# Six output tiles in place of four, under a fixed order of tasks

## The chip, the cores and the metric

The kernel runs on one core of one Trainium2 chip. The metric is the device time of one execution in microseconds (us), of which the median over several runs is taken. A span inside a profile runs from the first to the last instruction of the program.

## The reference

Attention over four batches of eight heads, 768 positions of width 64, followed by a gated matrix product over the 3072 resulting rows.

```python
# per batch and head; block = 32, window = 16, nb = 24
k_sum = k.reshape(B, H, nb, block, D).max(axis=3)
v_sum = v.reshape(B, H, nb, block, D).mean(axis=3)
scores_l = scale * q @ k.T                    # kept where |i - j| < window
scores_s = scale * q @ k_sum.T + log(block)   # 24 block summaries, always kept
a = softmax(concat([scores_l_masked, scores_s]))
x = a @ concat([v, v_sum])                    # to [3072, 512]
out = maximum(x @ w1, x @ w2) @ w_out         # 512 -> 1024 -> 512
```

The last line is computed in another form: with `wd = w2 - w1`, max(x w1, x w2) w_out is x (w1 w_out) + relu(x wd) w_out. The kernel forms the product w1 w_out once (tile `w1o`).

## The kernel before

The program is written as a list of about 680 *tasks*. A task is one operation, or one short run of matmuls, on one engine: a load or store (SP's DMA queue), a cast, a run of transposes, a copy out of PSUM. Tasks are registered by `op` in the order of the Python code and get numbers by that. Nothing is emitted then. The string `ORDER` is the written-out result of an earlier planning: each word is a letter for the engine (P TensorE, A ScalarE, D VectorE, G GpSimd, S SyncE), a task's number, and, after a colon, the slots of the buffers that the task is the first to write. `Plan.run` walks through the string and emits each task as it comes. The durations given to `op` are a planner's costs; `run` does not read them, except to see which engines may do a task.

Two consequences matter. An engine executes its own tasks strictly in the order of the string. Between engines, the layer beneath sets the waits, from what has been recorded *earlier* in the string: a task waits for earlier-recorded tasks that wrote what it reads, or that use the buffer it overwrites. So the order in which two tasks of different engines stand in the string decides which of them may have to wait for the other when they touch the same buffer.

Buffers come from `Ring`s. A ring is a number of equal slots; the word in `ORDER` says which slot a new buffer takes. The ones that matter here:

- `osr`: the output tiles `o`, [128, 512] in f32. One task "copy out" (ScalarE or VectorE, line 685, emitted at line 410) fills a tile from PSUM; one task "store" (lines 692 and 694) sends it to the output over SP's DMA queue, on which the loads of k, q and v stand too.
- `banks`: the eight PSUM banks. A group of scores (`scores`, matmuls at line 501) takes two adjoining banks, one for each of its two heads' halves; so do a pair of k and q transposes ("turn", line 434), the values (line 543) and the transposes of x (line 575). A hidden or output product takes one.
- `kqb`, `kx`, `qx`, `pb`, `g`, `land`: casts of k and q, their transposed forms, the exponentials, the rectified hidden rows, and the landing tiles of loads.

The work of a batch: load k, q, v into `land`; cast to bf16; transpose k and q on TensorE (L434); place them ("place k", "place q", copies at L410 from PSUM); block maxima of k on VectorE (L454); scores (L501); exponential on ScalarE (L515); mask on VectorE (L509); values (L543), normalised on VectorE (L549, L552); transposes of x (L575). `maxout` then does, for each group of 256 rows, four hidden products (L660) with their relu (L406 or L408) and two or three output products of 128 rows each (L674 with `w1o`, then L681 twice with `wo`), copied out and stored. The string weaves the products of one batch between the attention of the next, so that TensorE has work while the other engines prepare.

Each core's SP queue works in order: a store is issued when the DMAs ahead of it in the queue have been issued.

Of the kernel before, what the change touches and what calls it, by code (L numbers as in the profile page):

```python
# [12 lines left out]
F32 = mybir.dt.float32  # L13
# [8 lines left out]
    "G32:0,0 S39:0 P79:0,0 G7 G8 D81:0,0 P70:2,0 A92:2 S14:4 G9 A72:2,0 D82:0 P94:4,0 G101:3 S16:5 "  # L22
    "A96:1,0 D3 G10 D83 P103:6,0 S42:6 A69:0 D97:1 G102:1 P71:0 S43:7 A76:0 D84 P104:0 D98 D73:0 G78:2 "
    "A109:1 D105:3,0 G93:3 P80:0 A85:2 D75 P95:0 D74 D106:0 A100:3 P86:2 S62:1 P90:6 D99 A87:0 D107 D108 "
    "P88:0 P110:4 A91:1 D15:0,0 D18 P24:2 A89:2 D20 S52:3 P114:6 D21 A22 D19 A25 P112:0 A111:3 D17:0 "
    "S65:0 D26 A28 P33:3 D27 P116:4 D29 A34 A115:4 D30 P126:2 D31 S53:2 D35 A113:5 G45:0 D117:0 P121:6 "
    "D118:0,0 A49:1 D122:1 G48:0 P119:0 D127:2 D123:1,0 P46:4 S146:4,0 A120:0 D128:0 P124:6 A47:1,0 P50:0 "
    "D125 P131:2 D44:0 A64:0 P460:6 S147:0 D51:0 G63:0 P458:7 A461:0 D132:0 P446:4 D55:1 A59:0 D133:0 "
    "P449:5 S150:5,0 D459 P60:0 P56:2 P455:6 D61:0 A57:0 D66:0 P136:0 P452:7 D67:0 S153:6,0 D137:1 P456 "
    "D138:0 S152:0 P134:2 P129:0 D58:0 P447 S151:0 P453 D54:0 A448:0 S154:7 A130:1 P450 D135 G218:0 "  # L30
    "S156:1 A219:1 P464:4 D457:0 G163:1,0,0,0 G245:2 A451:0 D454:0 S148:0,0 P221:0,0 P139:2 P220:0 P476:6 "
    "D11:0 A140:2 D465 S149:0 A222:0,0 P462:5 D477:1 G257:3 A226:0 P480:7 D223:1 G258:1 A246:0 P482:2 "
    "D224 D463 A481 P141:3 D225 P259:0,0 A483 S175:2,0 P260:0 P227:5 D261:2,0 P478:7 A228:0 D142:2 P484:2 "
    "D143:0 A479 G155:0,0 P248:5,0 D262:0 P247:0 P144:3 A253:2 P471:7 D265:1 S170:3,0 A249:1,0 P485 D229 "
    "A145 P472 D263 D251 D250:1 G157:0 P486 P500:0 D487:0 G230:3 S161 P164:1 P489:5 A231:1 S174:0 D160 "
    "S162 A165 P494:6 D159 A501:2 A167 P232:3,0 P233:0 D264 P490 A234:3,0 D166 G187:0,0,0,0 D168 S169 "
    "A238:3 P473 D235:0 S173:4,0 A495 P496:2 S171:0 D236 D252 D237 D474:1 P266:0 A497 P242:3 P491 D158 "
    "S178:6 A243:2 S180:5 P498:6 D492:2 A267:3 S172:0 P239:2 D499 P269:4 P502:7 A240:5 S493 D268 P507:0 "
    "D244 A270:1 D241 P503 D271 P272:1 P284:3 P254:5 D273:0 D285:1 P504 D274:2,0 S176:7,0 A255:4 D286:0,0 "
    "P508 A505:3 D256 P275:1 A295:0 P278:5 G179:0,0 P287:3 D276:2 P466:7 D279:0 A307:2 D277:0 D288:1 P509 "  # L40
    "S177:0 D280:0 G294:3 D289:0 P281:1 G321:1 P467 S475 D282:2 D283:0 S201:1,0 G181:0 P296:5,0 A510:2 "
    "P290:3 P297:0 A298:0,0 P292:1 D291:3 S197:0,0 P468 A302:0 G306:3 D293 P188:0 S200:0 G322:0 P309:3,0 "
    "P323:5,0 S511 P308:0 A469:1 P516:1 D310:3,0 A325:2,0 S506 P514:2 G334:2 D191 A517:1 D311:1 P518:7 "
    "G333:1 A314:3 S194:6,0 D515 G186 P512:1 A519 S184 D185 P335:3,0 P324:0 A513 P336:0 D326:0 P536:2 "
    "S195:0 A329:1 D341:2 S199:3,0 P520:7 A189 A337:1,0 D313 P530:1 S183 D192 A537:2 D312 D339 D327 "
    "P532:5 D328 A531 D338:1 S198:0 A190 P330:3 P315:1 D300 P521 D299:0 G370:3 A316:0 P552:6 D340 D301 "
    "A331:3 D317 P522 D182 A553:0 P525:0 A523:2 D332 P303:1 A533 P345:3 D193 S204:5 P548:6 A304:5 S488 "
    "S196:0 P534:7 A549 S524 D305 P543:5 A535 P318:1 P342:6 P544 A319:2 P526 A343:1 D320 S202:4 P545 "
    "A346:4 S470 D344 P527 A546:3 P357:1 P351:6 A528:0 P354:3 P550:5 D352:0 A371:1 D355:1 S529 D353:1,0 "
    "P538:0 D358:2 G382:0 A551 D359:2,0 A383:2 P554:6 G205:0,0 D356:0 P561:7 A555 D347 P372:1,0 P385:3,0 "  # L50
    "P373:0 A374:2,0 P384:0 G409:3 P562 D378:1 A386:0,0 G397:2 P360:5 D390:0 P348:1 A410:1 P563 G203:0 "
    "D349:0 D361:2 D350:0 P556:3 D564:2 G211:1,0,0,0 S208 G209 P363:1 P557 D362:0 S206 S547 D364:1 P539 "
    "D365:0 P411:4,0 D387:1 P366:6 G207 P412:0 P368:1 A367:0 P558 D369 P540 A398:0 D559:1 P584:6 A413:3,0 "
    "S560 G210 S565 P568:7 A417:3 D585:1 P588:1 D376 D541:0 P602:2 D375:0 S542 P566:3 D569:0 A603:2 D377 "
    "P586:6 D567 P590:4 D389 A587 D414:0 P212:5 P379:2 D214 P400:6,0 D589 P399:0 A380:3 P604:0 D401:1,0 "
    "P570:1 A405:2 D381 P572:2 A213 D388 A605 D402:1 P574:3 A571 D573 A591 P592:6 D216 A215 D403 D404 "
    "P575 D415 D416 D217 P421:0 P394:4 P579:7 A422:0 P576 A395:2 P580 D577:3 P391:0 D396 S578 P406:4 "
    "P418:2 P593 A407:1 P581 A419:5 D408 P594 A582:1 D420 P597:4 A392:4 D423 P606:5 A595:2 D393 P598 A607 "
    "P433:2 P439:0 P424:6 D434:0 P599 D435:0,0 D440:2 P608:5 D425:1 A600:0 D426:1,0 P610:2 D441:0 A609 "
    "P436:3 P427:6 P430:0 P615:5 D428:0 D437:1 D429:0 P611 D438:0 D431:2 P616 D432:0 P444:6 P442:3 A445:3 "  # L60
    "P617 D443 P612 P674:0 D613:3 P644:1 S614 P628:3 A645:0 S601 P660:4 A618:3 P622:6 S619 S583 P669:7 "
    "D623:1 P624:2 P620:1 A625 P664:5 D621 P638:6 P640:2 D639 P626:1 D661:2 D641 P658:6 D627 P633:4 A659 "
    "P642:2 P634 D643 P662:1 P651:6 D663 P646:2 P656:1 P652 A657 P635 P665 A636:0 P653 P629 D654:3 P666 "
    "S655 S637 P647 A667:1 P630 S668 S596 P648 D631:3 P675 S632 A649:0 P670 P676 S650 P671 A677:1 D672:2 "
    "S678 S673 "
)

# [35 lines left out]
class Plan:  # L103
# [8 lines left out]
    def op(self, engine, us, fn, read=(), write=(), change=(), touch=(), behind=(), prio=0.0, label="",  # L112
           port=False, lanes=(0, 1)):
        t = Task()
        t.port, t.lanes = port, lanes
        t.engine, t.us, t.fn, t.label = engine, us, fn, label
        t.on = us if isinstance(us, dict) else {engine: us}
        t.prio = (prio, len(self.tasks))
        t.new, t.behind = [*write, *change], behind
        t.deps = {w for b in (*read, *change) for w in b.writers}  # L120
        for b in t.new:
            b.writers.append(t)
        for b in (*read, *touch, *t.new):
            b.users.append(t)
        self.tasks.append(t)
        return t
# [20 lines left out]
def kernel(  # L147
# [14 lines left out]
    nc = tc.nc  # L162
# [11 lines left out]
    op = plan.op  # L174
# [4 lines left out]
    def tiles(name, n, shape, dt):  # L179
        return [const.tile(shape, dt, name=f"{name}{i}") for i in range(n)]  # L180
# [18 lines left out]
    xtr = Ring(list(range(2 * NG)))  # L199
    xt_tile = const.tile([128, 2 * NG, KC, GT], BF16, name="xt")  # L200
    gr = Ring(tiles("g", 3, [128, FC, GT], BF16))
    osr = Ring(tiles("o", 4, [128, d_model], F32))
    wd = [Buf(Ring([t])) for t in tiles("wd", 4, [128, KC, 256], BF16)]
    w1br = Ring(tiles("w1b", 2, [128, KC, 256], BF16))
    w1b = [Buf(w1br) for _ in range(4)]
# [114 lines left out]
    def load_v(b, prio, gap, on):  # L320

        vb, parts = Buf(vbr), [Buf(Ring([None])) for _ in range(2)]
        vx_part[b] = [Buf(Ring([None])) for _ in range(2)]
        for n in range(2):
            f = Buf(land)
            view = lambda f=f: f.ap[:, 0:1536].rearrange("p (h m d) -> p h m d", h=4, d=D)
            op("SP", 3.6, lambda view=view, n=n: nc.sync.dma_start(
                out=view().rearrange("p h m d -> p (h m) d"),
                in_=v[b, 4 * n:4 * n + 4].rearrange("h (m r) d -> r (h m) d", r=128)),
               write=[f], behind=v_spread[b - 1], prio=prio + gap * n, label=f"load v{b}{n}")  # L330
            copy(on, lambda view=view, n=n: (
                vb.ap[:, :, 4 * n:4 * n + 4, 0:D].rearrange("p m h d -> p h m d"), view()),
                 read=[f, amean_in], write=[vb, parts[n]], prio=prio + 1, label=f"cast v{b}{n}")
        return vb, parts
# [259 lines left out]
    def load_w12(half, prio, prio_t):  # L594
        fs = []
        for w in (moe_w1, moe_w2):
            f = Buf(land)
            fs.append(f)
            op("SP", 2.75, lambda f=f, w=w: nc.sync.dma_start(
                out=wide(f), in_=w.rearrange("(c p) n -> p c n", p=128)[:, :, 512 * half:512 * half + 512]),  # L600
               write=[f], prio=prio, label=f"load w{half}")
        for n in (2 * half, 2 * half + 1):
            split_w12(n, fs, prio + 10 * (n % 2), prio_t)
# [22 lines left out]

    def load_wo(half, prio):
        f = Buf(land)
        op("SP", 2.75, lambda: nc.sync.dma_start(
            out=wide(f), in_=moe_w_out.rearrange("(c p) n -> p c n", p=128)[:, 4 * half:4 * half + 4, :]),  # L630
           write=[f], prio=prio, label=f"load wo{half}")
        for i in range(2):
            copy({"ACT": 1.05, "POOL": 1.05, "DVE": 0.65}, lambda i=i: (wo[2 * half + i].ap[:], wide(f)[:, 2 * i:2 * i + 2]),
                 read=[f], write=[wo[2 * half + i]], prio=prio + 400, label=f"wo {2 * half + i}")
# [147 lines left out]
```

## Time and profile before

| what | before |
|---|---|
| median of 4 runs | 173.05 us (172.38 to 173.88) |
| the profiled execution | 172.57 us |
| its span | 170.8 us |
| TensorE (PE) busy | 148.4 us, 87% |
| VectorE (DVE) busy | 113.1 us, 66% |
| ScalarE (ACT) busy | 92.1 us, 54% |
| GpSimd (POOL) busy | 42.5 us, 25% |
| mean granted TensorE clock | 0.987 |
| copies into `o` | 14 on ScalarE, 11 on VectorE |
| stores of 128 rows, 256 KB | median 2.5 us from issue to landing |

"Busy" is the time in which an engine executes; idle time of an engine costs something only where another one waits for it. The profile's chain of waits starts at the last instruction and goes back, at each step, to what released it. Views in order of time give the start, the length, the engine and line, the tiles written and read, and in brackets the idle time before and what ended it.

### The profile page before, as it was taken

The page shows a single profiled execution, that of the slowest core. Times are in us where ns is not written, and L with a number is a line of the kernel's source. Part 1 is how long each engine was busy: PE and PEld are TensorE (multiplying, and loading weights), DVE is VectorE, ACT ScalarE, POOL GpSimd, SP SyncE. Part 2 cuts the span into 40 slices and gives each one's busy share as a digit, 9 for nine tenths or more (in the row PEclk, how much of TensorE's full clock was granted, in tenths as well). Part 3 has the DMA queues.
Part 4 walks back from the last instruction along what each step waited for, and adds up shares of the span by engine and source line. Part 5 has one row for each costly group of instructions (what it writes and reads, how often), then busy time and mean ns, then how long its engine had stood idle before and what let it go on. Part 6 is the DMA issues. An engine that isn't in the chain of part 4 may idle for free.

```text
span 170.8 us, 5170 instructions
## 1 busy us (share of the span) xinstructions
PE 148.4 (87%) x2229; PEld 98.2 (57%) x2256; DVE 113.1 (66%) x204; ACT 92.1 (54%) x126; POOL 42.5 (25%) x63
## 2 busy tenths in 40 slices
PE   0237948999999999989899989999999999999992
PEld 0125626647846656567665654788556657876451
DVE  1647899689796887769996549488965661353110
ACT  3287997518764787087797860826666232110220
POOL 7643036106353002880100559500000000000000
PEclk9999996999999999999999999999999999999998
DMA  5998999999999699999999914640010003300065
GB/s 170 367 312 163 285 401 387 384 378 349 215 283 308 126 294 220 290 347 356 268 212 278 273 48 95 165 135 6 0 65 0 0 4 123 127 0 0 0 246 184
DMA packets 42071, 33.57 MB, mean 197 GB/s; under 512 B 25889, under 2 KB 36033, under 8 KB 42049
## 3 DMA queue, kind: packets, MB, share of 16 engines
q1 hardware_dynamic: 42048, 33.25, 68.5%
q8 instruction: 17, 0.28, 0.7%
q14 instruction: 6, 0.04, 0.1%
HBM read 25.17 MB, written 6.29 MB: 184 GB/s over the span
## 4 chain that ended last, share of the span: by engine, by line
PE 68%; DMA 16%; DVE 5%; ACT 4%; issue 3%; SPq 2%; POOL 0%; ACTq 0%; POOLq 0%
PE banks L681 22%; PE banks L660 20%; PE banks L674 11%; DMA land<-in_moe_w_dram 7%; DMA land<-in_q_dram 6%; PE banks L501 4%; PE banks L543 3%; PE banks L644 3%; DMA out_dram<-o 3%; PE banks L434 3%; SPq L305 2%; ACT kx L410 1%; PE banks L575 1%; DVE ks L454 1%; ACT pb L515 1%
## 5 line engine op out<-in xcount | busy, mean ns | idle before, releaser
L660 PE MATMUL banks<-xt,wd 128*128 128x256 bf16 x384 | 46.7, 274 | 0.1
L681 PE MATMUL banks<-wo,g 128*128 128x512 bf16 (+1 forms) x185 | 42.5, 370 | 1.9 <-issue 1.7
L660 PEld LDWEIGHTS <-wd 128*128 128x128 bf16 x384 | 37.2, 98 | 8.2
L515 ACT ACTIVATE pb<-banks,bias 128x1024 bf16<-128x1024 f32 x24 | 25.6, 1111 | 7.7 <-PE banks L501 6.9
L681 PEld LDWEIGHTS <-g 128*128 128x128 bf16 x200 | 18.4, 98 | 18.6
L406 ACT ACTIVATE g<-banks 128x512 bf16<-128x512 f32 x29 | 16.9, 598 | 20.7 <-PE banks L660 20.5
L410 POOL CAST kqb<-land 128x768 bf16<-128x768 f32 x19 | 16.4, 878 | 34.2 <-DMA land<-in_k_dram 28.6
L674 PE MATMUL banks<-w1o,xt 128*128 128x512 bf16 (+1 forms) x90 | 23.5, 370 | 0.6 <-issue 0.2
L434 PE MATMUL banks<-identity,kqb 64*128 64x64 bf16 x384 | 10.6, 202 | 11.9 <-DVE kx L236 4.7
L408 DVE TENSOR_SCALAR g<-banks 128x512 bf16<-128x512 f32 x19 | 12.8, 687 | 10.9 <-PE banks L660 10.9
L454 DVE TENSOR_REDUCE ks<-kx 128x24 bf16<-128x768 bf16 x16 | 15.1, 947 | 4.0 <-ACT kx L410 3.9
L434 PEld LDWEIGHTS <-kqb 64*128 64x128 bf16 x384 | 7.8, 101 | 15.6 <-ACT kqb L410 4.8
L410 ACT COPY o<-banks 128x512 f32<-128x512 f32 (+1 forms) x14 | 8.0, 571 | 15.4 <-PE banks L681 9.1
L552 DVE TENSOR_TENSOR xs<-banks,inv 128x512 bf16<-128x512 f32 x24 | 15.8, 679 | 0.3
L410 DVE COPY o<-banks 128x512 f32<-128x512 f32 (+1 forms) x11 | 7.3, 665 | 12.8 <-PE banks L681 11.7
L410 ACT CAST kqb<-land 128x768 bf16<-128x768 f32 x12 | 9.9, 835 | 9.3 <-DMA land<-in_k_dram 5.6
L509 DVE TENSOR_TENSOR pb<-pb,mask 128x1024 bf16<-128x1024 bf16 x18 | 12.0, 687 | 3.3 <-ACT pb L515 3.1
L674 PEld LDWEIGHTS <-xt 128*128 128x128 bf16 x100 | 9.3, 98 | 7.7
L410 POOL CAST vb<-land 128x1536 bf16<-128x1536 f32 x6 | 8.8, 1469 | 19.6 <-PE banks L543 14.6
L543 PEld LDWEIGHTS <-pb 128*64 128x64 bf16 x384 | 7.7, 112 | 7.8 <-issue 7.8
L543 PE MATMUL banks<-vx,pb 128*64 128x65 bf16 x384 | 9.5, 198 | 3.0 <-DVE vx L410 1.0
L410 ACT COPY qx<-banks 128x768 bf16<-128x768 bf16 x12 | 9.7, 805 | 2.6 <-PE banks L434 2.1
(66 smaller groups left out, 149.6 us busy)
## 6 DMA issues: line engine op xcount, KB each, us to landing
land<-in_k_dram SPq DMA_DIRECT2D x16, 384.0 KB, 7.0
land<-in_q_dram SPq DMA_DIRECT2D x16, 384.0 KB, 7.4
land<-in_v_dram SPq DMA_DIRECT2D x8, 768.0 KB, 11.1
out_dram<-o SPq DMA_DIRECT2D x19, 256.0 KB, 2.5
land<-in_moe_w_dram SPq DMA_DIRECT2D x4, 1024.0 KB, 10.4
land<-in_moe_w_out_dram SPq DMA_DIRECT2D x2, 1024.0 KB, 12.5
out_dram<-o SPq DMA_DIRECT2D x4, 224.0 KB, 3.1
vx<-vb SPq DMA_DIRECT2D x2, 396.0 KB, 7.0
```

The costliest lines, as they stand in the source:

```text
L406: nc.scalar.activation(out=o, in_=i, func=ACT.Relu)
L408: nc.vector.tensor_scalar_max(out=o, in0=i, scalar1=0.0)
L410: {"DVE": nc.vector.tensor_copy, "ACT": nc.scalar.copy, "POOL": nc.gpsimd.tensor_copy, "SP": nc.sync.dma_start}[e](out=o, in_=i)
L434: nc.tensor.transpose(out=bank(ps, 2048, BF16)[:, at:at + 64], in_=src.ap[r, j].rearrange("p h d -> p (h d)"), identity=identity[r, r])
L454: op("DVE", 0.95, lambda: nc.vector.tensor_reduce(out=ks.ap[:].rearrange("p (t s) -> p t s", s=2), in_=kt()[:, :, 0:64].rearrange("p t (s ...
L509: nc.vector.tensor_tensor(out=o, in0=o, in1=m, op=ALU.mult)
L515: op("ACT", 1.13, lambda: nc.scalar.activation(out=pb.ap[:].rearrange("p a n -> p (a n)"), in_=bank(ps, 1024), func=ACT.Exp, bias=bias[:], ...
L543: nc.tensor.matmul(out=av()[64 * par:64 * par + 64, c, 2 * u + a, :], lhsT=pb.ap[:, a, at:at + 64], rhs=vx[b].ap[:, 4 * grp + 2 * u + par, ...
L552: op("DVE", 0.69, lambda: nc.vector.tensor_tensor(out=x.ap[:, grp] if g1 == grp else x.ap[:, grp:g1 + 1, hp % 2], in0=av()[:, :, :, 0:D], ...
L660: nc.tensor.matmul(out=bank(ps)[:, 256 * s:256 * s + 256], lhsT=wd[n].ap[:, c, 128 * s:128 * s + 128], rhs=x_rows(b, grp)[:, c, :], start= ...
L674: nc.tensor.matmul(out=bank(ps, hi - lo), lhsT=x_rows(b, grp)[:, c, sl], rhs=w1o[c].ap[:, lo:hi], start=(c == 0), stop=False)
L681: nc.tensor.matmul(out=bank(ps, hi - lo), lhsT=g.ap[:, f, sl], rhs=wo[f // 2].ap[:, f % 2, lo:hi], start=False, stop=(f == FC - 1))
```

## The change

The ring `osr` gets six tiles in place of four (2 KB more on each partition for each of the two). `ORDER` is written anew: the tasks of each engine, taken alone, stand in the same order as before, but the slots of the output tiles differ, and so do some slots of `banks`, `kqb` and `kx`; and at a number of places tasks of different engines have changed places with one another in the string. Three planner costs are written differently.

```diff
-    osr = Ring(tiles("o", 4, [128, d_model], F32))
+    osr = Ring(tiles("o", 6, [128, d_model], F32))
...
-            op("SP", 3.6, lambda view=view, n=n: nc.sync.dma_start(
+            op("SP", 3.6 + 0.65 * n * (b == 0), lambda view=view, n=n: nc.sync.dma_start(
...
-            op("SP", 2.75, lambda f=f, w=w: nc.sync.dma_start(
+            op("SP", 2.85, lambda f=f, w=w: nc.sync.dma_start(
...
-        op("SP", 2.75, lambda: nc.sync.dma_start(
+        op("SP", 2.85, lambda: nc.sync.dma_start(
```

Two stretches of `ORDER`, the first around the copy A510 ("copy out 021") and the placement A298 ("place k20") with the transposes P297 ("turn q20"), the second around three groups of scores, P391, P406 and P418, and the exponentials of the latter two, A407 and A419:

```diff
-    "S177:0 D280:0 G294:3 D289:0 P281:1 G321:1 P467 S475 D282:2 D283:0 S201:1,0 G181:0 P296:5,0 A510:2 "
-    "P290:3 P297:0 A298:0,0 P292:1 D291:3 S197:0,0 P468 A302:0 G306:3 D293 P188:0 S200:0 G322:0 P309:3,0 "
+    "D280:0 S177:0 G294:3 D289:0 P281:1 G321:0 A510:4 P467 S475 D282:2 D283:0 S201:1,0 P296:5,0 G181:0 "
+    "P290:3 A298:0,0 P297:0 P292:0 D291:3 S197:0,0 P468 A302:0 G306:3 D293 P188:2 S200:0 A469:5 G322:1 "
...
-    "P575 D415 D416 D217 P421:0 P394:4 P579:7 A422:0 P576 A395:2 P580 D577:3 P391:0 D396 S578 P406:4 "
-    "P418:2 P593 A407:1 P581 A419:5 D408 P594 A582:1 D420 P597:4 A392:4 D423 P606:5 A595:2 D393 P598 A607 "
+    "P575 D415 D416 D217 P421:0 P394:3 P579:7 A422:0 P576 A395:2 P580 D577:5 P391:0 D396 S578 P406:3 "
+    "A407:1 P418:2 D408 P593 A419:5 P581 D420 P594 A582:4 D423 A392:4 P597:5 P606:4 A595:1 D393 P598 A607 "
```

## The prediction

> **What bounds the kernel now.** I read the busy shares first, then the chain of work that ended last, then the waits on the tile that the change touches, then single engines in order of time where they meet.
>
> ```profile
> PE 148.4 (87%) x2229; PEld 98.2 (57%) x2256; DVE 113.1 (66%) x204; ACT 92.1 (54%) x126; POOL 42.5 (25%) x63
> PE   0237948999999999989899989999999999999992
> DMA  5998999999999699999999914640010003300065
> PE 68%; DMA 16%; DVE 5%; ACT 4%; issue 3%; SPq 2%; POOL 0%; ACTq 0%; POOLq 0%
> ```
>
> TensorE is the bound. It is full from slice 7 (30 us) to slice 38; the transfers are full until about 98 us, hidden behind it except at the start. A change pays only where it moves TensorE. The waits name three in which ScalarE could not write an output tile, because the store of its last content had not landed:
>
> ```profile
> ACT o L410 <- DMA out_dram<-o: 6.1, 3, 4.3
> ```
>
> The chain, in order of time (start, length, what), runs through the longest:
>
> ```profile
> 67.80 4.68 DMA out_dram<-o
> ...
> 72.56 0.04 ACT o L410
> ...
> 73.04 0.81 ACT kx L410
> 73.84 0.71 ACT qx L410
> 74.56 0.04 issue
> 74.60 0.54 PE banks L434 x24
> ```
>
> This invites the reading that 4.68 us hang on the store. But the chain is followed back from TensorE's last wait alone; what TensorE did meanwhile is in the next view, TensorE from 69 to 75 us (start, length, line, and in brackets its idle time before):
>
> ```profile
> 70.98 0.35 PE L434 MATMUL banks<-identity,kqb 64*128 64x64 bf16 x12
> 71.17 0.51 PE L575 MATMUL banks<-identity,xs 64*128 64x64 bf16 x24
> 71.52 0.34 PE L434 MATMUL banks<-identity,kqb 64*128 64x64 bf16 x12
> 72.37 0.81 PE L681 MATMUL banks<-wo,g 128*128 128x512 bf16 x3 [0.16 <-issue]
> 73.65 0.35 PE L434 MATMUL banks<-identity,kqb 64*128 64x64 bf16 x12
> 74.60 0.53 PE L434 MATMUL banks<-identity,kqb 64*128 64x64 bf16 x24 [0.60 <-ACT qx L410]
> ```
>
> TensorE worked through ScalarE's 4.31 us wait and lost 0.60 us at its end. That 0.60, not 4.68, is what the store costs here. The other two waits, at 75.36 (0.81 us) and 144.46 (1.01 us), have no idle TensorE beside them.
>
> **The change, part by part.** *Six tiles.* The 25 output copies and the stores are the same ones in the same order on their engines. The fifth and sixth copies take fresh tiles, and later ones reuse a tile that was stored two turns earlier, so all three waits go. Nothing is added on DVE, POOL or SP; the stores stay queued on SP behind the same loads, so transfers do not start earlier.
>
> *The two planner costs* (3.6, 2.75) are written but not used when the order is replayed: nothing.
>
> *The list.* For each engine taken alone the task numbers stand in the same order. But two things moved with the tiles: the slots of some PSUM banks, and which engine's task is recorded first. Both make waits. I compared each instruction's waits in the two built programs; where the replaced producer had finished long before, the change costs nothing, as TensorE or its feeder hides it. Two places remain.
>
> *Place one, 70 to 75 us.* "copy out 021" (A510) no longer waits: TensorE's group for it ends about 69.7, so it runs 69.75 to 70.35. "place k20" (A298) follows. It needs the transposes of k20, the first L434 row, done at 71.33, and takes 0.81: 71.4 to 72.2. Before, A298 was recorded after P297, the transposes of q20 into the same pair of banks; now it is recorded ahead, so P297 waits for A298's read. That is a new wait. P297 stood at 71.52 and goes to 72.25: +0.73. Queued behind it on TensorE are the second x transposes (L575), four output matmuls (L681), the means (L346) and the transposes at 73.65, all 0.7 late. The next group, at 74.60, waited 0.60 for "place q20" on ScalarE. That copy can now start when P297 ends, 71.88 + 0.73 = 72.6, and ends about 73.45, so it binds no more; the group simply follows the one before it, which overlaps as 71.17 overlaps 70.98 (0.16 us): 74.00 - 0.16 + 0.70 = 74.54 against 74.60. So the freed 0.60 is eaten by the new wait. Bounds: -0.8 if P297 did not wait at all, +0.2 if nothing overlaps. I take -0.1. The k and q placements on DVE from 75.17 to 83.45, then the scores at 83.50, all start from that 74.60 group and move with it.
>
> *Place two, 126 us.* Three groups of scores stand back to back on TensorE (L501 x48, sixteen each: P391, P406, P418), then output matmuls:
>
> ```profile
> 125.53 0.87 PE L501 MATMUL banks<-qx,kx 64*128 64x64 bf16 x48
> 126.56 2.54 PE L681 MATMUL banks<-wo,g 128*128 128x512 bf16 x11 [0.16 <-issue]
> 126.21 2.12 ACT L515 ACTIVATE pb<-banks,bias 128x1024 bf16<-128x1024 f32 x2 [1.42 <-PE banks L501]
> 128.75 1.12 ACT L515 ACTIVATE pb<-banks,bias 128x1024 bf16<-128x1024 f32 x1
> ```
>
> Each group writes two adjoining banks. Before, P406 has slot 4 (banks 4, 5) and P418 slot 2 (2, 3). Now P406 has slot 3 (banks 3, 4), and P418 still 2 and 3: they share bank 3, and P418 must wait until the exponential of P406 (A407) has read it. Its first matmul goes to bank 2; the second is the one that waits. A407 starts when P406 is done, 126.21, takes 1.12, ends 127.33; TensorE reacts 0.04 later (74.56 to 74.60 above): 127.37. P418 stood at 125.53 plus two groups: 36 such matmuls took 0.67 at 58.38 and 48 take 0.87 here, so sixteen cost 0.27, and it stood at 126.06. The new wait is 1.3 us. Queued behind it are the output matmuls of P593, P581, P594 and all that follows, though their inputs are ready. From here to the end TensorE has no wait to give it back: from 128 to 163.5 it is busy 34.97 of 35.50 us. The end, copies and stores, follows the last matmul as before. Bounds: 1.1 if the shift is partly taken by the remaining 0.53 of idle, 1.5 if the sixteen matmuls lose their overlap.
>
> *Does the stall cost more than itself?* The granted clock over three stretches of 3.4 us (the second number is the length, the third TensorE's busy time; its clock stands right of POOL's busy time):
>
> ```profile
> 23.10:26.50 3.40, 0.92 (x24) 0.61 (x23) 3.27 (x6) 3.38 (x4) 2.02 (x2) 1.00 1.04 389
> 26.50:29.90 3.40, 3.07 (x69) 2.51 (x70) 3.40 (x8) 2.14 (x4) 1.97 (x2) 0.50 1.06 390
> 81.10:84.50 3.40, 2.69 (x50) 2.14 (x50) 3.15 (x10) 2.36 (x5) 0.82 (x1) 1.00 1.08 283
> ```
>
> After 2.48 us idle the next 3.4 us ran at half clock; after 0.71 idle nothing fell. The stretch from 125.5 would hold 1.3 + 0.16 = 1.5 us idle, between the two and nearer the harmless one, so I take no further cost; the bound above is half clock for 3.4 us, which loses 1.7.
>
> "TensorE: Matmul & The Clock Gate", section HAM oscillation, of the Trainium skill warns of idle gaps over about 3.4 us. The trace differs: the clock fell although the longest gap in that stretch was 1.00 us. By the rule the sum stays at +1.2; by the rows it may be +2.9, where the clock falls.
>
> *Sum.* -0.1 + 1.3 = +1.2 us. The profiled execution took 172.57 us (span 170.8 and 1.8 around it), so 173.8; it lies 0.48 under the median of the runs, 173.05, on which the forecast is 174.2. A measurement of this kernel tells about 1% (1.7 us) from no change, so +1.2 is no change.
>
> **The rivals.**
>
> *Faster: the store's segment was on the path.* If all 4.68 us of it come back and the later wait is paid, 173.05 - 4.68 + 1.3 = 169.7. For it: the chain. Against: TensorE was busy 7.27 of the 8.10 us from 67.0 to 75.1, so there are 0.83 to win. Chance 0.08.
>
> *Nothing reaches the end.* If the stall at 126 is hidden, as when the exponential's read frees the bank early: 173.05. Against: matmuls start in order and the wait stands in the built program. Chance 0.12.
>
> *Slower: the stall at 126 lowers TensorE's clock.* 174.2 + 1.7 = 175.9. It decides from some idle time between 0.71 and 2.48 of 3.4 us. For it: the half clock after 26.5. Against: 1.5 us idle lies nearer the harmless stretch, and dense matmuls follow at once. Chance 0.15.
>
> **How the numbers follow.** Forecast 0.65, rivals 0.08, 0.12 and 0.15. The forecast's own range, with the bounds of both places (-0.8 to +0.2, 1.1 to 1.5) and the spread of runs (172.38 to 173.88), is 172.8 to 175.2; about a third of its weight passes the 1% line at 174.8. With the clock rival and the second inside, 172.7 to 176.1; the faster rival is left out. Slower: 0.20 of the forecast and the clock's 0.15, with 0.01 from the second rival: 0.36. Faster 0.08. Same 0.56.
>
> **What would show it.** ScalarE's three waits on stores are gone. At place one TensorE idles some 0.6 us ahead of the second L434 group, released by the k placement, and no more ahead of the third. At 126 us a gap of 1.3 us appears inside the L501 group, ended by L515, with TensorE full behind it. The forecast is wrong if TensorE reaches 100 us more than 0.8 us earlier, if that gap is missing, or if the clock falls after it.

## The result and the profile after

| | before | changed |
|---|---|---|
| median | 173.39 us (172.05 to 175.49, 61 runs) | 174.23 us (173.06 to 176.21, 42 runs) |
| ratio of the changed kernel to before | | 1.0052, 95% interval 1.0035 to 1.0068 |
| profiled execution, its span | 172.57, 170.8 us | 174.91, 173.1 us |

The changed kernel is about 0.9 us longer, 0.5%: no change by the 1% line, as forecast, and on the side that was forecast. The ratios here and below leave out runs that lie over 1.5% above the fastest run of their kernel; the profiled execution of e5, 178.70 us, is such a run.

The page of the changed kernel: TensorE by slices, and the chain by engines.

```profile
PE   0449349999999999899899989999969999999992
PE 71%; DVE 12%; DMA 8%; issue 2%; SPq 2%; ACT 2%; DVEq 0%; ACTq 0%
```

A 6 stands now in slice 29 of TensorE's row, 126 to 130 us, where a 9 stood. Transfers have half their former share of the chain. The store of the output tile, 2.7% of the span before, is no longer on it, and the loads at the start have 8.3% where they had 12.8%, so most of the difference lies in the start. Of the waits for an `o` tile on ScalarE, none names a store any more; what is left, but for 0.2 us, is this line (total, times, longest), the wait for the product itself:

```profile
ACT o L410 <- PE banks L681: 11.6, 8, 2.9
```

Place one, TensorE in order of time, then ScalarE:

```profile
72.09 0.35 PE L434 MATMUL banks<-identity,kqb 64*128 64x64 bf16 x12
72.27 0.51 PE L575 MATMUL banks<-identity,xs 64*128 64x64 bf16 x24
73.33 0.35 PE L434 MATMUL banks<-identity,kqb 64*128 64x64 bf16 x12 [0.54 <-ACT kx L410]
...
75.38 0.70 PE L434 MATMUL banks<-identity,kqb 64*128 64x64 bf16 x36
76.01 3.67 PE L660 MATMUL banks<-xt,wd 128*128 128x256 bf16 x32
```

```profile
70.84 0.58 ACT L410 COPY o<-banks 128x512 f32<-128x512 f32 x1 [1.49 <-PE banks L681]
72.48 0.80 ACT L410 COPY kx<-banks 128x768 bf16<-128x768 bf16 x1 [1.05 <-PE banks L434]
73.72 0.80 ACT L410 COPY qx<-banks 128x768 bf16<-128x768 bf16 x1 [0.44 <-PE banks L434]
```

The output copy runs as soon as its product is there. The placement of k follows its transposes. Then TensorE waits 0.54 us for that placement ahead of the second L434 group, a wait that it did not have. The 0.60 that it lost ahead of the third group is gone: the last 36 transposes are one unbroken group. One wait has taken the place of the other.

Place two, TensorE and ScalarE:

```profile
126.48 0.67 PE L501 MATMUL banks<-qx,kx 64*128 64x64 bf16 x33
128.33 0.39 PE L501 MATMUL banks<-qx,kx 64*128 64x64 bf16 x15 [1.18 <-ACT pb L515]
128.88 2.54 PE L681 MATMUL banks<-wo,g 128*128 128x512 bf16 x11 [0.16 <-issue]
```

```profile
127.17 1.11 ACT L515 ACTIVATE pb<-banks,bias 128x1024 bf16<-128x1024 f32 x1 [1.42 <-PE banks L501]
128.76 1.11 ACT L515 ACTIVATE pb<-banks,bias 128x1024 bf16<-128x1024 f32 x1 [0.48 <-PE banks L501]
```

The 48 score matmuls are cut after 33: two groups of sixteen and the first matmul of P418, the one that goes to bank 2. The 34th, to bank 3, waits until the exponential of P406 ends at 128.28. The two exponentials that ran back to back before stand apart.

To compare kernels whose starts differ, I cut the trace at four points of TensorE's order that all kernels have: the weight loads at the start of the first L434 group of place one, of the L660 group behind place one, of the three score groups, and of the L681 group behind them. The last column goes on from there to the last L681 weight load; "start" is the time of the first point, the others are lengths. Times in us:

| profile | start | place one | to the scores | place two | to the last |
|---|---|---|---|---|---|
| before | 70.98 | 4.08 | 50.47 | 0.81 | 40.85 |
| before, second profile (e8) | 71.59 | 4.26 | 50.16 | 0.80 | 40.85 |
| changed | 72.08 | 3.93 | 50.47 | 2.17 | 40.85 |
| six tiles, old list (e1) | 71.68 | 3.20 | 50.17 | 0.81 | 40.85 |
| changed, banks apart (e2) | 72.53 | 3.92 | 50.20 | 0.80 | 40.85 |
| before, bank shared (e3) | 72.27 | 4.45 | 50.16 | 2.17 | 40.85 |
| changed, turn first (e4) | 71.43 | 3.20 | 50.17 | 2.17 | 40.85 |
| four tiles, new list (e5) | 72.47 | 7.51 | 50.17 | 2.17 | 40.84 |
| changed, exponential twice (e6) | 72.07 | 3.93 | 50.16 | 3.31 | 40.85 |
| changed, three times (e7) | 71.49 | 3.93 | 50.16 | 4.47 | 42.52 |

The two spans differ by 2.3 us, but 1.1 of that lies ahead of 72 us. From the first point to the last it is 96.21 against 97.42: +1.2.

A gap costs more than the idle time in its bracket. Place two is 1.36 us longer for an idle time of 1.18 in the changed kernel, and 2.50 and 3.66 longer for 2.33 and 3.47 in e6 and e7; place one is 0.73 longer than in e1 for 0.54. That is 0.17 to 0.19 more each time. Unbroken groups overlap in the rows (the one at 72.27 starts 0.17 before the end of the one at 72.09, which takes 0.35); across a gap that overlap is lost, and it is about as large as the difference.

### The profile page after: what moved, and what is told of

Read it like the earlier page. It is cut to its first block, busy times and chain, and to the rows that moved or that the text cites. A ratio compares the mean times of both kernels' runs of the same rounds, so it can differ in the third digit from the quotient of the medians.

```text
span 173.1 us, 5171 instructions
## 1 busy us (share of the span) xinstructions
PE 149.3 (86%) x2229; PEld 98.7 (57%) x2256; DVE 114.8 (66%) x204; ACT 92.2 (53%) x126; POOL 43.8 (25%) x63
## 4 chain that ended last, share of the span: by engine, by line
PE 71%; DVE 12%; DMA 8%; issue 2%; SPq 2%; ACT 2%; DVEq 0%; ACTq 0%
PE banks L681 22%; PE banks L660 22%; PE banks L674 10%; DMA land<-in_v_dram 8%; PE banks L644 4%; PE banks L543 4%; DVE vx L410 3%; PE banks L501 3%; PE banks L434 2%; SPq L305 2%; DVE ks L454 2%; PE banks L575 2%; DVE qx L410 2%; ACT kx L410 1%; DVE kx L410 1%
## 5 line engine op out<-in xcount | busy, mean ns | idle before, releaser
L660 PE MATMUL banks<-xt,wd 128*128 128x256 bf16 x384 | 47.9, 279 | 0.1
L681 PE MATMUL banks<-wo,g 128*128 128x512 bf16 (+1 forms) x185 | 42.5, 370 | 1.9 <-issue 1.7
L660 PEld LDWEIGHTS <-wd 128*128 128x128 bf16 x384 | 37.7, 100 | 8.7
L681 PEld LDWEIGHTS <-g 128*128 128x128 bf16 x200 | 18.4, 98 | 18.6
L410 POOL CAST kqb<-land 128x768 bf16<-128x768 f32 x19 | 17.2, 915 | 31.5 <-DMA land<-in_k_dram 25.5
L408 DVE TENSOR_SCALAR g<-banks 128x512 bf16<-128x512 f32 x19 | 12.8, 688 | 11.0 <-PE banks L660 10.9
L434 PE MATMUL banks<-identity,kqb 64*128 64x64 bf16 x384 | 10.4, 202 | 9.7 <-DVE kx L236 4.9
L434 PEld LDWEIGHTS <-kqb 64*128 64x128 bf16 x384 | 7.8, 101 | 13.4 <-DVE kx L236 4.9
```

Of the source, the lines that this page charges most:

```text
L408: nc.vector.tensor_scalar_max(out=o, in0=i, scalar1=0.0)
L410: {"DVE": nc.vector.tensor_copy, "ACT": nc.scalar.copy, "POOL": nc.gpsimd.tensor_copy, "SP": nc.sync.dma_start}[e](out=o, in_=i)
L434: nc.tensor.transpose(out=bank(ps, 2048, BF16)[:, at:at + 64], in_=src.ap[r, j].rearrange("p h d -> p (h d)"), identity=identity[r, r])
L660: nc.tensor.matmul(out=bank(ps)[:, 256 * s:256 * s + 256], lhsT=wd[n].ap[:, c, 128 * s:128 * s + 128], rhs=x_rows(b, grp)[:, c, :], start= ...
L681: nc.tensor.matmul(out=bank(ps, hi - lo), lhsT=g.ap[:, f, sl], rhs=wo[f // 2].ap[:, f % 2, lo:hi], start=False, stop=(f == FC - 1))
```

## The experiments

The theory: more tiles help a little at place one; the list that came with them costs at both places. The main rivals: the difference lies in the tiles' addresses or the start, or the store's 4.68 us was on the path.

**e1: the tiles alone.** Six tiles and the changed kernel's slots for `o`; every other word of the list as before.

```diff
-    osr = Ring(tiles("o", 4, [128, d_model], F32))
+    osr = Ring(tiles("o", 6, [128, d_model], F32))
...
-    "... P296:5,0 A510:2 P290:3 P297:0 A298:0,0 P292:1 ..."
+    "... P296:5,0 A510:4 P290:3 P297:0 A298:0,0 P292:1 ..."
```

> Six tiles, the list of the kernel before in every other word (its PSUM slots, its order between engines). Theory (the tiles help a little, the list costs at two places): the waits of ScalarE on stores go, the turn of q20 no longer waits for the placement of k20 (in the changed kernel it does), so the L434 group that stood at 74.60 us comes 0.7 us earlier against the work before it, and the L501 x48 group at 126 us runs unbroken. 0.7 us less than before: ratio 0.996, and about 1.6 us less than the changed kernel. Rival (the two tiles themselves, by where they put the other tiles in SBUF, or the run's start make the 0.9 us that the changed kernel is longer): ratio 1.005, as the changed kernel. Rival (the store's 4.68 us segment was on the path): ratio 0.973.

Measured: 172.74 us median, ratio to before 0.9959, interval 0.9930 to 0.9988. TensorE at the two places:

```profile
71.87 0.51 PE L575 MATMUL banks<-identity,xs 64*128 64x64 bf16 x24
72.22 0.34 PE L434 MATMUL banks<-identity,kqb 64*128 64x64 bf16 x12
...
74.26 0.70 PE L434 MATMUL banks<-identity,kqb 64*128 64x64 bf16 x36
...
125.06 0.87 PE L501 MATMUL banks<-qx,kx 64*128 64x64 bf16 x48
```

No idle time at place one at all, and the scores unbroken. The same six tiles that came with a slower kernel make a faster one: the tiles' addresses and their number are not the cost. The rival of the store falls as well: with it off the path the kernel gained 0.7 us, not 4.7. This version is the shortest of the three: its interval, 0.9930 to 0.9988, lies below 1 and does not meet that of the changed kernel, 1.0035 to 1.0068.

**e2: the changed kernel with the banks apart.** From P406 on, the old PSUM slots and the old order between engines, with the new `o` slots.

```diff
-    "... P391:0 D396 S578 P406:3 A407:1 P418:2 D408 P593 A419:5 P581 ... P597:5 P606:4 ..."
+    "... P391:0 D396 S578 P406:4 P418:2 P593 A407:1 P581 A419:5 D408 ... P597:4 ... P606:5 ..."
```

> The changed kernel, but from the scores P406 on with the PSUM slots and the order between engines of the kernel before: P406 takes banks 4 and 5 again and shares none with P418. Theory: the gap of 1.18 us inside the L501 group at 128 us goes, 1.36 us less than the changed kernel, so 0.1 to 0.2 under the kernel before: ratio 0.999. Rival (the 0.9 us come from the tiles' places or the start): ratio 1.005 still.

Measured: 173.25 us, ratio 0.9997 (0.9966 to 1.0028). Place two is 0.80 us long, place one 3.92 as in the changed kernel. The stall is what made the changed kernel longer than before.

**e3: the kernel before with the bank shared.** The reverse: four tiles, the changed kernel's PSUM slots and order from P406 on.

```diff
-    "... P391:0 D396 S578 P406:4 P418:2 P593 A407:1 P581 A419:5 D408 ..."
+    "... P391:0 D396 S578 P406:3 A407:1 P418:2 D408 P593 A419:5 P581 ..."
```

> The kernel before with four tiles, but from P406 on with the PSUM slots and order of the changed kernel: P406 on banks 3 and 4, P418 on 2 and 3. Theory: the stall alone, with everything ahead of it as before: a gap of about 1.2 us in the L501 group at 126 us, TensorE full behind it, 1.36 us more at the end: ratio 1.008. Rival (the tiles' places or the start make the difference): ratio 1.000.

Measured: 175.28 us, ratio 1.0113 (1.0071 to 1.0155); the expected 1.008 lies in the interval. The gap came with these slots and this order alone, under four tiles. No run took the order apart from the slots; where P406 and P418 share no bank, it gives them nothing to wait for. TensorE in e3:

```profile
126.89 0.67 PE L501 MATMUL banks<-qx,kx 64*128 64x64 bf16 x33
128.74 0.39 PE L501 MATMUL banks<-qx,kx 64*128 64x64 bf16 x15 [1.18 <-ACT pb L515]
```

**e4: the changed kernel with the turn first.** Two words exchanged; no slot and no engine's own order differs.

```diff
-    "P290:3 A298:0,0 P297:0 P292:0 D291:3 ..."
+    "P290:3 P297:0 A298:0,0 P292:0 D291:3 ..."
```

> The changed kernel with two words of its list exchanged: the transposes of q20 (P297) stand ahead of the placement of k20 (A298) again, as before. Theory: the idle 0.54 us ahead of the second L434 group at 73 us goes and the L434 group that stood at 74.60 us comes about 0.6 us earlier than in the changed kernel; the stall at 126 us stays: ratio 1.002. Rival (place one hides behind other work): as the changed kernel, ratio 1.005.

Measured: 173.26 us, ratio 1.0017 (0.9981 to 1.0053). The median alone would not separate it from the changed kernel. The trace does: place one 3.20 us against 3.93, to the hundredth what e1 has, and place two as in the changed kernel. So 0.73 us at place one hang on which of two words stands first. One of the two tasks waits for the other in either order: in e1 the placement starts at 72.60, when both runs of transposes are done (72.22 + 0.34), in the changed kernel at 72.48, after the first alone (72.09 + 0.35). With the turn first it is ScalarE that waits, and TensorE loses nothing by it.

**e5: the list without the tiles.** The changed kernel's list with four tiles and the old `o` slots.

```diff
-    osr = Ring(tiles("o", 6, [128, d_model], F32))
+    osr = Ring(tiles("o", 4, [128, d_model], F32))
...
-    "... G321:0 A510:4 P467 ..."
+    "... G321:0 A510:2 P467 ..."
```

> Four tiles, but the changed kernel's list in all else (its PSUM slots, its order between engines). Theory: both costs of the list without the help of the tiles. The copy of output 021 waits for its store again, the placement of k20 follows it, and now the turn of q20 waits for that placement: in the kernel before that placement ended at 73.85, so the turn goes from 71.52 to 73.9, and the L434 group at 74.60 goes to about 76.2, 1.6 us later; the stall of 1.36 us at 126 us comes on top. About 3.0 us more than before: ratio 1.017. Rival (the store's wait does not reach TensorE under either list): only the stall, ratio 1.008.

Measured: 177.62 us, the median of four runs from 175.89 to 178.70; ratio 1.0187 (1.0112 to 1.0261), beside the expected 1.017. In the profiled execution, the longest of the four, place one took 7.51 us, more than the expected 5.7. ScalarE and TensorE, then two stretches with the clock:

```profile
74.51 0.58 ACT L410 COPY o<-banks 128x512 f32<-128x512 f32 x1 [4.77 <-DMA out_dram<-o]
75.84 0.35 PE L434 MATMUL banks<-identity,kqb 64*128 64x64 bf16 x12 [2.68 <-ACT kx L410]
73.30:76.60 3.30, 0.70 (x36) 0.69 (x37) 0.87 (x1) 1.65 (x3) 2.17 (x3) 1.00 1.05 396
76.70:80.00 3.30, 3.28 (x64) 1.88 (x64) 0.91 (x1) 1.10 (x3) 0.92 (x2) 0.50 1.06 389
```

The store landed later than in the profile of before (4.77 us of waiting against 4.31), and now the whole wait reaches TensorE: copy, placement, turn. After 2.60 of 3.30 us idle the clock fell to half. Against e1's place one of 3.20 us, the turn comes 2.84 us later behind the first point (3.37 against 0.53), and from the turn to the L660 group it takes 4.13 against 2.67, 1.46 more at half clock. The second part need not be there in each run: the mean granted clock was 0.958 in this and one other run, 0.969 and 0.971 in the remaining two. Under this list the two tiles more are worth some 2.3 us (1.0187, with its wide interval, against 1.0052), under the old one 0.7.

**e6 and e7: the exponential of P406 twice and three times.** The same values are written again.

```diff
+            for _ in range(2 if tag == "3 20 21" else 1):
+                nc.scalar.activation(out=pb.ap[:]..., in_=bank(ps, 1024), func=ACT.Exp, ...)
```

> The changed kernel with the exponential of P406 (A407) done twice, into the same tile; everything else as it was. Theory: the gap inside the L501 group at 128 us is as long as that exponential, so it grows by the second one's 1.0 to 1.1 us, from 1.18 to about 2.25, and the whole by as much: ratio 1.012. Clock rival: with 2.4 us of 3.4 idle TensorE's granted clock falls to half for 3.4 us and adds up to 1.7 us more: ratio 1.021. Rival (the gap has another cause than this exponential): as the changed kernel, 1.005.

> The same exponential done three times. Theory: a gap of about 3.3 us at 128 us, 2.1 to 2.2 us more than in the changed kernel between the start of the L501 group and the L681 group behind it. Clock rival: after so long a gap (before, 2.48 us of idle time in 3.4 us were followed by half clock) the granted clock falls to 0.5 behind the gap and the L681 and L660 matmuls there take twice as long for 3.4 us.

Measured: e6 176.20 us, ratio 1.0150 (1.0100 to 1.0200); e7 178.03 us, a single run. The gaps, of e6 and of e7:

```profile
129.16 0.39 PE L501 MATMUL banks<-qx,kx 64*128 64x64 bf16 x15 [2.33 <-ACT pb L517]
```

```profile
129.73 0.39 PE L501 MATMUL banks<-qx,kx 64*128 64x64 bf16 x15 [3.47 <-ACT pb L517]
```

1.18, 2.33, 3.47: the gap grows by 1.15 and 1.14 with each exponential, so it is the exponential's length that sets it. The clock: two stretches each of the changed kernel, of e6, and of e7.

```profile
126.40:129.80 3.40, 2.06 (x54) 1.38 (x55) 1.40 (x3) 2.16 (x2) 0.00 (x0) 1.00 0.22 82
129.80:133.20 3.40, 3.40 (x21) 1.90 (x20) 1.99 (x3) 2.16 (x5) 0.00 (x0) 1.00 0.00 0
```

```profile
124.80:128.10 3.30, 2.03 (x40) 1.01 (x39) 1.70 (x3) 1.85 (x3) 0.00 (x0) 1.00 0.21 79
128.20:131.50 3.30, 2.19 (x24) 1.23 (x25) 1.46 (x3) 2.10 (x3) 0.00 (x0) 1.00 0.02 5
```

```profile
126.60:130.00 3.40, 0.27 (x15) 0.27 (x14) 0.29 (x1) 3.01 (x3) 0.00 (x0) 1.00 0.15 55
130.10:133.40 3.30, 2.97 (x9) 1.14 (x9) 1.60 (x3) 1.11 (x1) 0.00 (x0) 0.50 0.02 5
```

The changed kernel kept the full clock after its gap, and so did e6 after 2.33 us. In e7 it fell to 0.50 for one stretch, and the rest of the kernel took 42.52 us against 40.85, 1.67 more: the price that the prediction put on that rival, 1.7, at a gap nearly three times as long as the change's.

**e8: the kernel before once more,** without an edit, for a second profile.

> The kernel before once more, for a second profile of it. Theory: the stretch from the first L434 group at 70.98 us to the L660 group at 75.06 us, 4.08 us in the first profile, is longer in some executions, as the store that ScalarE waits for lands at a time that the transfers set (4.45 in the run with one shared bank, whose list is the same up to there); the stretch from the scores at 126 us to the end stays the same. Rival: it is 4.08 again, and the 4.45 came from the other list.

Measured: 173.04 us, one run; place one 4.26 us. With 4.08 and the 4.45 of e3 that makes three values for one list up to there, while the changed list without a store to wait for gave 3.93, 3.92, 3.93, 3.93. ScalarE's copy that waits for the store starts 1.58, 1.76 and 1.96 us behind the first point (72.56, 73.35 and 74.23), so place one grows by what the store lands later, within 0.01 us. Why the store lands later is not shown.

## Why the prediction was right, point by point

*What bounds.* Right, but the price was too small. The store's 4.68 us in the chain were not worth 4.68: without them (e1) 0.7 us came back in the median. They were not worth 0.60 either: e1's place one is 0.88 us shorter than that of the same profile, and 1.06 shorter than the mean of the three with the old list, as a gap costs more than its bracket and the store often lands later. The bound of -0.8 for a P297 that does not wait was too near for the same reason; e4 shows that case, 0.88 below the profile of before. A chain that is followed back from an engine's last wait does not tell what that engine did meanwhile; TensorE's own rows did.

*The planner costs.* Nothing was seen of them, and no run took them out alone.

*Place one.* The mechanism was right in each step: the new wait of 0.54 us ahead of the second group, released by the placement of k, and the 0.60 us ahead of the third gone. P297 went from 0.54 us behind the first point to 1.24, +0.70 where +0.73 was forecast. The term was -0.1; between the two profiles it is -0.15. Against the mean of the three profiles with the old list, 4.26, it is -0.33: the store landed at another time in each of the three, and the profile of before has the shortest place one of them. This term was sized on one execution; the forecast held because it is small beside place two. With -0.33 and the +1.36 of place two the sum is +1.0, which is 1.006 and inside the interval; the forecast of +1.2 is 1.0069 and just above it.

*Place two.* Forecast 1.3, measured 2.17 - 0.81 = 1.36, alike in the changed kernel, e3 and e4. The remainder of the kernel, 40.85 us, gave nothing back.

*The range.* The bounds and the spread of runs add up to 172.7 to 175.6 us (172.38 - 0.8 + 1.1 and 173.88 + 0.2 + 1.5), not to 172.8 to 175.2. The result, 174.23, lies within both.

*The rivals.* The faster one fell with e1. The second, that the stall is hidden, fell with e2 and e3. The clock rival's price was right and its place was real, as e5 and e7 show, but 1.18 us of idle time were too few. The margin was small: 1.81 us of idle time in 3.40 were enough in the start of e7, as the last section shows, so the 1.5 us that the prediction reckoned with were not safely harmless, and that the clock held is partly luck. The clock fell after a gap of 3.47 us in e7, of 2.68 in e5, and in the start of the kernel before with none over 1.00: what counts in these rows is how much of a stretch was idle. The rule of "TensorE: Matmul & The Clock Gate" in the Trainium skill, section HAM oscillation, is no idle gaps over about 3.4 us. It agrees with the first of these three and not with the others, so the measurements go before it.

*What was not in the prediction.* The start, up to the first point, took between 70.98 and 72.53 us over the ten profiles. The changed list has 72.0 on average and the old one 71.6; with that spread it stays open whether the list has a part in it. Half clock at the start lasted 3.41 us in the profile of before and 10.24 in that of the changed kernel, which may be part of the 1.1 us between them; in the other eight it lasted 6.83 or 10.24 and does not order the starts (71.59 to 72.53 and 71.43 to 72.47).

## What to carry to other kernels

A larger ring of buffers is not a change of that ring alone where a written-out list or a planner hands out other buffers and fixes which instruction is recorded first: here six tiles were worth -0.4% by themselves and +0.5% with the list that came along. Before such a change is judged, compare the waits of each instruction in the two programs, look only at those whose new producer ends late, and check whether neighbours on the bounding engine now share a buffer. A wait that heads the chain is worth about the time that the bounding engine loses beside it (0.60 us idle in the row, 0.88 between the cut points), not its own length (4.31).

## What the runs showed of the hardware

*The length of a gap alone does not tell whether the clock falls.* A gap of 2.33 us (e6) left the clock at 1.00, one of 2.68 (e5) halved it for 3.4 us, and before, 2.48 us of idle time in gaps of at most 1.00 did so too. In the clock records of all ten traces each stay at half clock before the end of the work lasts 3.41, 6.83 or 10.24 us, that is one, two or three steps of 3.41. Counted in such steps from the changes of the clock at the start of the same trace, the gap of e6 lies over two stretches, each over 60% busy (its two rows above, with e6), while in e5 and e7 one stretch held 2.60 and 3.13 us of idle time. That the share of a fixed stretch decides fits all of these. How large it must be is narrowed by the starts of e6 and e7, a stretch of each and the one behind it:

```profile
18.94:22.34 3.40, 2.02 (x61) 1.50 (x58) 2.35 (x4) 2.34 (x2) 0.00 (x0) 1.00 0.94 329
22.35:25.75 3.40, 0.82 (x29) 0.64 (x24) 3.29 (x6) 3.35 (x5) 1.38 (x1) 1.00 1.03 378
```

```profile
17.43:20.83 3.40, 1.59 (x47) 1.14 (x46) 2.51 (x4) 2.01 (x4) 0.00 (x0) 1.00 0.58 189
20.84:24.24 3.40, 2.68 (x39) 1.83 (x39) 3.32 (x5) 3.34 (x4) 1.21 (x1) 0.50 1.06 399
```

After 1.38 us of idle time in e6 the clock stayed at 1.00, after 1.81 in e7, with no gap over 1.84, it fell. So from full clock the limit lies between 1.4 and 1.8 us idle of 3.4 in these ten traces.

*Small VectorE copies that meet a GpSimd cast take longer.* The same copy into `kx` (L461, 128 x 288) took 0.86 us in the profile of before, where it started beside a cast on GpSimd, and 0.23 in e1, where the cast came later and a copy at L458, 0.16 elsewhere, took 0.71 in its place. Before, then e1:

```profile
82.58 0.86 DVE L461 COPY kx<-ks 128x288 bf16<-128x288 bf16 x1
...
82.53 0.82 POOL L410 CAST kqb<-land 128x768 bf16<-128x768 f32 x1 [5.63 <-DMA land<-in_k_dram]
```

```profile
82.41 0.23 DVE L461 COPY kx<-ks 128x288 bf16<-128x288 bf16 x1
...
83.42 0.71 DVE L458 COPY kx<-kx 128x32 bf16<-128x32 bf16 x1
...
83.28 0.82 POOL L410 CAST kqb<-land 128x768 bf16<-128x768 f32 x1 [5.44 <-DMA land<-in_k_dram]
```

Each of the slow copies ended within 0.1 us of the cast's end (83.44 after 83.35, 84.13 after 84.10). In nine of the ten profiles the cast starts when a load lands, so it falls on another copy in each execution; in e4, e5 and e7 it met none of these copies, and all of them took their usual times (0.22 or 0.23 us at L461, 0.16 or 0.17 at L458). Before, it delayed a copy that the scores at 83.50 wait for, and in the changed kernel one that its scores at 84.45 wait for: the stretch to the scores took 50.47 us in both, 50.20 in e2, where it reached such a copy for a moment, and 50.16 or 50.17 elsewhere. So it has no part in the difference between the two profiles.

The page "SBUF — State Buffer" of the Trainium skill, section SBUF: two separate sides, says that GpSimd and VectorE instructions of certain kinds take turns at one pair of ports, the one that comes second waiting for the whole instruction of the other. The two ends above agree with that; no row tells of which kind these copies are, and no run took the cast away to test it.
